# Chunked attention and a squared-ReLU layer in one kernel: the halves of x swapped, transposes, loads and the last product put at other steps

## The chip, the cores and the metric

The kernel runs on one core of a Trainium2 chip. The metric is the device time of one execution in microseconds, as a median over runs. Five engines work beside each other: TensorE (PE; its weight loads are listed as PEld), VectorE (DVE), ScalarE (ACT), GpSimd (POOL), and SyncE (SP), which here only issues transfers. Each engine takes its instructions strictly in the order of its own queue.

## The reference

Attention within chunks of 64 rows, then a feed-forward layer with a squared ReLU. Inputs and output are float32.

```
q, k, v: (8, 8, 576, 64)          # batch, heads, rows, width
scores = q_c @ k_c.T / 8          # inside each chunk of 64 rows
attn   = exp(scores - max) / sum
x      = (attn @ v_c), heads side by side    # (4608, 512)
h      = max(x @ w_in, 0)         # w_in (512, 2048)
out    = (h * h) @ w_out          # w_out (2048, 512), out (4608, 512)
```

## The kernel before

The 4608 rows are cut into 18 groups g of 256 rows and 9 blocks j of two groups (block j holds groups 2j and 2j+1). Groups 0 to 13, 16 and 17 are four neighbouring chunks of one batch; groups 14 and 15 (block 7) gather the last chunk of every batch, so their loads and stores come in more pieces. Everything is computed in bfloat16 with float32 sums.

The whole order is written out by hand. A table `plan` maps a step ("slot") to the functions that are called there; each engine's queue gets its instructions in the order of these calls. The work on one group has short names: its loads (`qk_pieces`, `v_pieces`, issued on SP), C(g) casts q and k to bfloat16 (L435, on POOL or ACT), TD(g) transposes them by one DMA on SP (L443), SC(g) makes the scores on PE and the exponential on ACT (L451), AV(g), or AV0(g) and AV1(g) for its two tiles, multiplies by V on PE and divides by the sums on DVE (L483, `out_of_x` L427: a reciprocal and a multiplication), and XT(g) transposes x into the block's tile `xT` (L517). XT is eight PE transposes and a copy up to group 11, and one DMA transpose on SP from group 12 on (`FIRST_DMA_X`). `xT` of a block has two halves of 256 rows; group 2j goes into half 0 and group 2j+1 into half 1.

Blocks 0 to 3 compute x @ w_in plainly (`ffn_in`, L559): 16 steps of four matmuls, each followed by a ReLU on ACT and a square on DVE or ACT. In block 2 the steps ("slots") 0 to 15 are these; AV(7) stood at slot 14, XT(6) after it at slot 14, XT(7) at slot 17. Slots 14 and 15 also hold the DVE sums of `g` for the second layer of block 2.

Blocks 4 to 8 use a scheme with seven products instead of eight, in quads Q (a quarter of the features of a block each): Q = 0 to 3 is block 4, Q = 12 to 15 block 7, Q = 16 to 19 block 8. Each tick of the loop `run` (L1125) has four steps s = 4*tick + i, so a block has 16 steps; block 7 begins at s = 48. The seven products of a quad are spread over two ticks:

```
groups = (((tick, "A1"), (tick - 1, "A7")), ((tick, "B2"), (tick - 1, "C3")),
          ((tick, "A6"), (tick - 1, "A4")), ((tick, "C5"),))
```

They read sums of the halves of x, which DVE makes (`x_sums`, L607): e1 is read by A1, e2 by A6, e3 by C5, e4 by A4; B2, C3 and A7 read x itself. With `xs(j, d, t)` for half t of x (d is the half of its features):

```
e1 = xs(j,0,1) - xs(j,1,1)      e2 = e1 + xs(j,0,0)
e3 = e2 - xs(j,1,0)             e4 = xs(j,0,1) + xs(j,0,0)
```

The sums of block j+1 are called in block j at its steps 13.5, 15, 17.5 and 18. e1 reads half 1 alone, e2 both halves.

The second layer is `ffn_out` (L713), also with seven products of 16 matmuls each; A and BC are its two accumulators. p1 multiplies a DVE sum d4 of `g` (d4 = g(0,1) - g(0,0)) by b21, p2 multiplies the plain piece g(0,0). The further DVE sums d5 (read by the third product), d3 (by the fourth) and d2 (by the seventh) are called after the half products K5, K2, K3 = 0, 1, 4. For blocks before the last the half products lie between the quads of the next block; those of the last block (the tail) run by themselves at the end. `keep` copies an accumulator away on ACT, `summed_out` (L801) adds on DVE and stores.

Block 6 calls, at its steps 0 to 14, one load each of block 8: six of q and k, then nine of V. It also calls XT(14) at 11.5, XT(15) at 12, C(16) and C(17) at 9 and 13, TD(16) and TD(17) at 12 and 13.5.

Of the kernel before, what the change touches and what calls it, by code (L numbers as in the profile page):

```python
# [144 lines left out]
def kernel(  # L145
# [22 lines left out]
    blocks = [[g, g + 1] for g in range(0, n_grp, 2)]  # L168
    n_blk = len(blocks)
# [7 lines left out]
    def is_whole(g):  # L177
        return chunks[g][0][0] == chunks[g][3][0]
# [5 lines left out]
    QUADS = 4  # L184
    LEAD = 4

    K5, K2, K3 = 0, 1, 4
    K5L, K2L, K3L = 2, 5, 5
# [97 lines left out]
    for g in range(n_grp):  # L286
        if is_whole(g):
# [3 lines left out]
            b, s = chunks[g][0]  # L291
# [47 lines left out]
    state = {}  # L339
    banks = {}  # L340

    def x_tile(j):
        if j not in xTs:
            xTs[j] = att_pool.tile([128, BT // 128, n_dt, 128], BF16, name="xT", bufs=2)
        return xTs[j]
# [170 lines left out]

    def transpose_x(g):  # L517
        x = state.pop(("x", g))
        dst = x_tile(g // 2)[:, g % 2 * 2:g % 2 * 2 + 2].rearrange("p t h q -> p (t h) q")
        if g >= FIRST_DMA_X:  # L520
            nc.sync.dma_start_transpose(out=dst, in_=x.rearrange("p t h a d -> p (t h a d)"))
            return
        psb = att_bank().bitcast(BF16)[:, 0:1024].rearrange("p (b q) -> p b q", q=128)
        for t in range(2):
            for hp in range(n_hp):
                nc.tensor.transpose(  # L526
                    out=psb[:, t * n_hp + hp, :],
                    in_=x[:, t, hp].rearrange("p a d -> p (a d)"),
                    identity=ident)
        copy = nc.vector.tensor_copy if g == blocks[1][0] else nc.scalar.copy  # L530
        copy(out=dst, in_=psb)  # L531
# [5 lines left out]
    for j in range(n_blk):  # L537
        if j < QUADS:
            at = {(th, fh, h): 4 * th + 2 * fh + h
                  for th in range(2) for fh in range(2) for h in range(2)}  # L540
        else:
# [6 lines left out]
            at = {(*key, 0): s for key, s in zip(keys, old)}  # L548
# [164 lines left out]
    def ffn_out(j):  # L713
# [4 lines left out]
        last = j == n_blk - 1  # L718
# [57 lines left out]
            return kept_sb[state["kept"] % 2]  # L776

        def store(dma, o_sb, half, col, t=None):
            g = blocks[j][half]
            b, s0 = chunks[g][0]  # L780
            t0 = b * S + s0
            if not is_whole(g):

                for p in range(2):
                    dma.dma_start(
                        out=out.rearrange("(b s) d -> s b d", s=S)[
                            s0:s0 + CH, b + p:b + 4:2, col:col + HD],
                        in_=o_sb[p * CH:(p + 1) * CH].rearrange("p (t d) -> p t d", d=HD))
            elif t is None:
                dma.dma_start(  # L790
                    out=out[t0:t0 + GT, col:col + HD].rearrange("(t p) d -> p t d", p=128),
                    in_=o_sb.rearrange("p (t d) -> p t d", d=HD))
            else:
                dma.dma_start(
                    out=out[t0 + t * 128:t0 + (t + 1) * 128, col:col + HD],
                    in_=o_sb[:, t * HD:(t + 1) * HD])
# [23 lines left out]
        def half(n):  # L820
            if early:
                return
            if n == (K5L if plain_first else K5):
                g_sum(d5, j, (1, 1), d4, ALU.subtract)
            if n == (K2L if plain_first else K2):
                g_sum(d2, j, (0, 1), (1, 1), ALU.subtract)
            if n == (K3L if plain_first else K3):
                g_sum(d3, j, (1, 0), d5, ALU.subtract)

        p1 = product(A, d4, b21, True)  # L830
        p2 = product(BC, (0, 0), b11_p_b21, True)
        order = (p2, p1) if plain_first else (p1, p2)
        for i, p in enumerate(order):
            for t in range(2):
                next(p)
# [142 lines left out]
    for j in range(QUADS):  # L978
        grps, nxt, far = blocks[j], blocks[j + 1], blocks[j + 2]
        plan = {}  # L980

        def at(slot, f, *x):
            plan.setdefault(slot, []).append((f, x))

        if j == 0:
            loads, go_slots = pieces(far), range(17)
            at(28, summed(b11_p_b21, b11, b21))
            for slot, f in ((24, TA), (27, SC), (29, AV), (31, XT)):
                at(slot, f, nxt[0])
            at(31, TQ, nxt[1])  # L990
            at(31, summed(b22_m_b21, b22, b21, ALU.subtract))
            phases = [first_ffn_in, ffn_out_by_ft(0)]
        elif j == 1:
            loads, go_slots = itertools.chain(*map(qk_pieces, far)), range(26, 48)
            for slot, f in ((1, TK), (4, SC), (7, AV), (12, XT)):
                at(slot, f, grps[1])
            for i, g in enumerate(nxt):
                for slot, f in ((16 + 4 * i, C), (21 + 4 * i, TD), (36 + i, SC), (38 + 2 * i, AV),
                                (41 + 2 * i, XT)):
                    at(slot, f, g)  # L1000
            for i, g in enumerate(far):
                at(36 + 4 * i, C, g)
                at(42 + 3 * i, TD, g)
            at(2, summed(b12_p_b21, b12, b21))
            at(12, summed(b11_m_b12, b11, b12, ALU.subtract))
            at(20, summed(b12_p_b22, b12, b22))
            out_j = ffn_out(1)
            for i in (20, 27, 29, 31):
                at(i, lambda: next(out_j)())
            phases = [ffn_in(1, [(0, 256, FT_ORDER), (256, 256, FT_ORDER)]), out_j]  # L1010
        else:
            out_j = ffn_out(j)
            for i in (14, 15):
                at(i, lambda: next(out_j)())
            phases = [ffn_in(j, [(0, BT, range(n_ft))])]
            if j == 2:
                loads, go_slots = itertools.chain(*map(v_pieces, nxt), pieces(far)), [
                    *range(16), *range(27, 36)]
                slots = {SC: (6, 9), AV: (11, 14), XT: (14, 17), C: (21, 26), TD: (25, 29)}
                for f in (C, TD):  # L1020
                    for i, g in enumerate(far):
                        at(slots[f][i], f, g)
                phases.append(out_j)
            else:
                loads, go_slots = pieces(far), range(11)
                for f, slots in ((C, (11, 13)), (TD, (13, 15))):
                    for i, g in enumerate(far):
                        at(slots[i], f, g)
                slots = {SC: (2, 4), AV: (7, 10), XT: (13, 15)}
            for f in (SC, AV, XT):  # L1030
                for i, g in enumerate(nxt):
                    at(slots[f][i], f, g)
            if j == 2:
                for i, f in enumerate((summed(a21_p_a22, a21, a22),
                                       summed(a12_m_a21, a12, a21, ALU.subtract),
                                       summed(a11_p_a21, a11, a21))):
                    at(1 + 2 * i, f)
        slot = 0
        for phase in phases:
            for _ in phase:  # L1040
                if slot in go_slots:
                    for f in loads:
                        f()
                        break
                for f, x in plan.get(slot, []):
                    f(*x)
                slot += 1
        assert all(x < slot for x in plan), (j, slot, sorted(plan))
        if j < QUADS - 1:
            go(loads)  # L1050
# [19 lines left out]
    for j in range(QUADS, n_blk):  # L1070
# [26 lines left out]
        if j + 1 < n_blk:  # L1097
            S0, V0, V1, X0 = ((1.5, 3.5), (4.5, 7.5), (6, 9.5), (8.5, 11.5)) if j == QUADS else (
                (0.5, 7), (2, 8), (3.5, 9.5), (3.5, 10)) if is_whole(blocks[j + 1][0]) else (
                (3.5, 9), (5, 10), (7, 11.5), (11.5, 12))  # L1100
            for i, g in enumerate(blocks[j + 1]):
                at(j, S0[i], SC, g)
                at(j, V0[i], AV0, g)
                at(j, V1[i], AV1, g)
                at(j, X0[i], XT, g)
            if j + 2 == n_blk:
                at(j, 22, check_sums)
                at(j, 25.5, count_bad)
            for i, s in enumerate((13.5, 15, 17.5, 18)):
                at(j, s, x_sums, j + 1, i)  # L1110
# [3 lines left out]
            assert next(loads, None) is None  # L1114
        if j + 2 < n_blk:
            more = pieces(blocks[j + 2])
            for s in range(0, 16):
                at(j, s, load, 1 if is_whole(blocks[j + 2][0]) else 2, more)
            for i in range(2):
                at(j, (9, 13)[i], C, blocks[j + 2][i])  # L1120
                at(j, (12, 13.5)[i], TD, blocks[j + 2][i])
    tail = ffn_out(n_blk - 1)
    at(n_blk, 3, lambda: next(tail)())

# [63 lines left out]
```

## Time and profile before

| | |
|---|---|
| median of 3 runs | 288.05 us (287.52 to 288.37) |
| profiled execution | 287.81 us, of it 286.0 us span |
| PE busy | 269.3 us (94%) |
| DVE, ACT, POOL busy | 199.1, 166.0, 91.8 us |
| mean granted PE clock | 0.991 |

The profiled execution is one run of the program on the chip. Its span goes from the first to the last instruction; 1.81 us lie around it. PE is nearly always busy, so an edit counts where it takes away or adds PE idle time, or time in which PE's clock is granted only in part. In the rows of the timeline view the columns are start, duration (from the first start to the last end of a merged run), engine, line, operation, destination and sources, and in brackets the idle time ahead of it and what ended it. SPq, POOLq and ACTq are the issue of a transfer, not its flight.

### The profile page before, as it was taken

To read this page: it belongs to the slowest core of one execution; us is meant where nothing else is said; L and a number is where in the kernel's file an instruction comes from. 1 tells how busy PE (TensorE), PEld (TensorE's weight loads), DVE (VectorE), ACT (ScalarE), POOL (GpSimd) and SP (SyncE) were. 2 spreads that over 40 slices of the span, in tenths; PEclk is the share of its full clock that TensorE was granted. 3 is DMA by queue.
4 is the path that set the end of the run, shared out by engine and by line. 5 is a ranking of instruction groups with operands and counts; after the bars stand their busy time and mean duration, and the time that the engine had idled before them with its cause. 6 is when DMAs were issued, how large, how long until landed. Compare 5 with 4: busy or idle time off the path is not lost.

```text
span 286.0 us, 7983 instructions
## 1 busy us (share of the span) xinstructions
PE 269.3 (94%) x3291; PEld 205.6 (72%) x3291; DVE 199.1 (70%) x367; ACT 166.0 (58%) x296; POOL 91.8 (32%) x123
## 2 busy tenths in 40 slices
PE   2999999999999799999999999999969999999994
PEld 2774445788764478447879888888847888888783
DVE  1276515999537671599989997789638877994841
ACT  1537614894458664875778666575626654766320
POOL 2047733240450001141245344522612322431612
PEclk9999999999999999999999999999988999999998
DMA  7999999989999976999998997798997320220313
GB/s 220 241 312 388 389 307 274 328 196 168 300 190 232 239 149 145 279 239 189 227 236 175 218 218 182 145 220 193 267 175 170 76 70 6 87 62 7 94 55 112
DMA packets 135480, 55.61 MB, mean 194 GB/s; under 512 B 104272, under 2 KB 131152, under 8 KB 135440
## 3 DMA queue, kind: packets, MB, share of 16 engines
q1 hardware_dynamic: 132432, 45.76, 69.3%
q0 software_dynamic: 2864, 9.18, 9.8%
q8 instruction: 27, 0.44, 0.6%
q10 hardware_dynamic: 144, 0.13, 0.1%
q14 instruction: 13, 0.11, 0.1%
HBM read 36.70 MB, written 9.44 MB: 161 GB/s over the span
## 4 chain that ended last, share of the span: by engine, by line
PE 81%; DVE 7%; DMA 4%; ACT 3%; SPq 3%; issue 1%; ACTq 0%
PE ps_ffn L642 20%; PE ps_out L761 19%; PE ps_ffn L565 15%; PE ps_ffn L761 13%; PE ps_ffn L877 5%; DMA qk_st<-in_k_dram 3%; DVE gT L583 2%; PE ps_att L470 2%; PE ps_att L497 2%; DVE x L432 2%; SPq L279 2%; PE ps_ffn L422 1%; PE ps_att L526 1%; DVE w_st L599 1%; PE ps_ffn L389 1%
## 5 line engine op out<-in xcount | busy, mean ns | idle before, releaser
L565 PE MATMUL ps_ffn<-xT,w_in_bf 128*128 128x512 bf16 (+1 forms) x328 | 58.7, 333 | 0.4 <-DVE xT L531 0.2
L761 PEld LDWEIGHTS <-w_st 128*128 128x128 bf16 x512 | 49.1, 98 | 8.3 <-DVE w_st L599 1.6
L650 DVE CUSTOM_DVE_ANT_0 relu<-ps_ffn,w_st 128x512 f32<-128x512 f32 x60 | 39.4, 684 | 14.5 <-PE ps_ffn L642 13.1
L583 DVE TENSOR_TENSOR gT<-relu 128x256 bf16<-128x256 bf16 (+2 forms) x69 | 33.7, 516 | 20.3 <-ACT relu L576 19.9
L576 ACT ACTIVATE relu<-ps_ffn 128x256 bf16<-128x256 f32 (+2 forms) x82 | 39.9, 503 | 11.7 <-PE ps_ffn L565 10.1
L565 PEld LDWEIGHTS <-w_in_bf 128*128 128x128 bf16 x328 | 30.9, 98 | 21.6 <-DVE xT L531 0.4
L642 PE MATMUL ps_ffn<-qk_st,w_in_bf 128*128 128x256 bf16 x240 | 35.3, 273 | 2.8 <-DVE qk_st L599 2.8
L790 POOL DMA_DIRECT2D out_dram<-o_sb x27 | 19.8, 733 | 53.1 <-DVE o_sb L599 52.0
L642 PEld LDWEIGHTS <-w_in_bf 128*128 128x128 bf16 x320 | 30.8, 98 | 7.3 <-DVE qk_st L599 3.1
L761 PE MATMUL ps_out<-w_out_bf,w_st 128*128 128x256 bf16 x240 | 31.0, 273 | 0.4 <-DVE w_st L599 0.4
L761 PEld LDWEIGHTS <-gT 128*128 128x128 bf16 x296 | 28.6, 98 | 3.4
L684 ACT ACTIVATE w_st<-ps_ffn 128x512 f32<-128x512 f32 x20 | 11.9, 597 | 25.8 <-PE ps_ffn L642 25.8
L481 ACT ACTIVATE e<-ps_att 128x1024 bf16<-128x1024 f32 x18 | 18.4, 1024 | 13.4 <-PE ps_att L470 13.4
L432 DVE TENSOR_TENSOR x<-ps_att,recs 128x512 bf16<-128x512 f32 x36 | 24.9, 691 | 1.2
L642 PEld LDWEIGHTS <-qk_st 128*128 128x128 bf16 x240 | 22.8, 99 | 3.1
L642 PE MATMUL ps_ffn<-xT,qk_st 128*128 128x256 bf16 x160 | 24.4, 277 | 0.0
L661 POOL TENSOR_TENSOR qk_st<-relu 128x512 bf16<-128x512 f32 x10 | 10.3, 1034 | 41.7 <-DVE relu L650 41.7
L661 POOL TENSOR_TENSOR gT<-relu 128x512 bf16<-128x512 f32 x10 | 10.3, 1034 | 41.4 <-DVE relu L650 37.6
L761 PE MATMUL ps_ffn<-w_out_bf,w_st 128*128 128x256 bf16 x144 | 17.6, 273 | 0.3 <-DVE w_st L599 0.3
L659 ACT ACTIVATE gT<-relu 128x512 bf16<-128x512 f32 x28 | 17.7, 633 | 0.0
L438 POOL CAST qkb<-qk_st 128x1024 bf16<-128x1024 f32 x12 | 12.6, 1048 | 15.0 <-DMA qk_st<-in_q_dram 15.0
L599 DVE TENSOR_TENSOR w_st<-gT,w_st 128x1024 bf16<-128x1024 bf16 x26 | 17.3, 700 | 0.0
(91 smaller groups left out, 430.8 us busy)
## 6 DMA issues: line engine op xcount, KB each, us to landing
qk_st<-in_q_dram SPq DMA_DIRECT2D x16, 512.0 KB, 5.4
out_dram<-o_sb POOLq DMA_DIRECT2D x31, 256.0 KB, 4.1
qk_st<-in_k_dram SPq DMA_DIRECT2D x24, 256.0 KB, 5.6
ve_sb<-in_v_dram SPq DMA_DIRECT2D x32, 128.0 KB, 4.0
w_st<-in_moe_w_in_dram SPq DMA_DIRECT2D x8, 512.0 KB, 6.5
w_st<-in_moe_w_out_dram SPq DMA_DIRECT2D x8, 512.0 KB, 5.5
vo_sb<-in_v_dram SPq DMA_DIRECT2D x24, 128.0 KB, 3.4
qk_st<-in_k_dram SPq DMA_DIRECT2D x4, 512.0 KB, 5.9
```

The costliest lines, as they stand in the source:

```text
L432: nc.vector.tensor_tensor(out=x, in0=o[:, :, :, 0:D], in1=rec.to_broadcast([128, 2, n, D]), op=ALU.mult)
L481: nc.scalar.activation(out=e_out, in_=s_in, func=AF.Exp, scale=scale)
L565: nc.tensor.matmul(out=h[:, 0:n], lhsT=w_in_bf[:, dt, ft * 128:(ft + 1) * 128], rhs=xT[:, c // 128:(c + n) // 128, dt, :], start=(dt == 0) ...
L576: nc.scalar.activation(out=rl[:, 0:n], in_=h[:, 0:n], func=AF.Relu)
L583: nc.vector.tensor_tensor(out=dst, in0=src, in1=src, op=ALU.mult)
L599: nc.vector.tensor_tensor(out=out, in0=in0, in1=in1, op=op)
L642: nc.tensor.matmul(out=bank[:, f * GT:(f + 1) * GT], lhsT=a[:, dt, ft * 128:(ft + 1) * 128], rhs=b[:, :, dt, :], start=(first and f == 0 a ...
L650: nc.vector._custom_dve(TENSOR_ADD_SAT, out=out, in0=in0, in1=in1, s0=BIG, s1=0.0)
L659: engine.activation(out=dst, in_=r, func=AF.Square)
L661: engine.tensor_tensor(out=dst, in0=r, in1=r, op=ALU.mult)
L761: nc.tensor.matmul(out=out_ps, lhsT=lhsT, rhs=b[:, i, :], start=(first and i == 0 and (last or t == 0)), stop=(i == HF - 1), skip_group_ch ...
L790: dma.dma_start(out=out[t0:t0 + GT, col:col + HD].rearrange("(t p) d -> p t d", p=128), in_=o_sb.rearrange("p (t d) -> p t d", d=HD))
```

## The change

`half_of(g)` puts group 2j into half 1 and group 2j+1 into half 0 from block 4 on; the stores follow. In block 2 AV(7) moves to slot 15, and XT(7) to slot 24. In block 6 XT(14) moves from step 11.5 to 7.5, TD(16) from 12 to 9.5, and the nine loads of V of block 8 from steps 6 to 14 to steps 10 to 15.5, two of them between TD(16) and XT(15), seven behind XT(15). In the last block p2 is computed ahead of p1, and d3 and d2 are called after the half products 4 and 5 (d2 before: 1).

```diff
+    def half_of(g):
+        return g % 2 if g // 2 < QUADS else 1 - g % 2
...
     def transpose_x(g):
         x = state.pop(("x", g))
-        dst = x_tile(g // 2)[:, g % 2 * 2:g % 2 * 2 + 2].rearrange("p t h q -> p (t h) q")
+        n = 2 * half_of(g)
+        dst = x_tile(g // 2)[:, n:n + 2].rearrange("p t h q -> p (t h) q")
...
         def store(dma, o_sb, half, col, t=None):
-            g = blocks[j][half]
+            g, = (g for g in blocks[j] if half_of(g) == half)
...
         def half(n):
             if early:
                 return
-            if n == (K5L if plain_first else K5):
+            k5, k2, k3 = (K5L, K2L, K3L) if plain_first else (0, 5, 4) if last else (K5, K2, K3)
+            if n == k5:
                 g_sum(d5, j, (1, 1), d4, ALU.subtract)
-            if n == (K2L if plain_first else K2):
+            if n == k2:
                 g_sum(d2, j, (0, 1), (1, 1), ALU.subtract)
-            if n == (K3L if plain_first else K3):
+            if n == k3:
                 g_sum(d3, j, (1, 0), d5, ALU.subtract)
...
-        order = (p2, p1) if plain_first else (p1, p2)
+        order = (p2, p1) if plain_first or last else (p1, p2)
...
             if j == 2:
-                slots = {SC: (6, 9), AV: (11, 14), XT: (14, 17), C: (21, 26), TD: (25, 29)}
+                slots = {SC: (6, 9), AV: (11, 15), XT: (14, 24), C: (21, 26), TD: (25, 29)}
...
             S0, V0, V1, X0 = ((1.5, 3.5), (4.5, 7.5), (6, 9.5), (8.5, 11.5)) if j == QUADS else (
                 (0.5, 7), (2, 8), (3.5, 9.5), (3.5, 10)) if is_whole(blocks[j + 1][0]) else (
-                (3.5, 9), (5, 10), (7, 11.5), (11.5, 12))
+                (3.5, 9), (5, 10), (7, 11.5), (7.5, 12))
...
             more = pieces(blocks[j + 2])
-            for s in range(0, 16):
-                at(j, s, load, 1 if is_whole(blocks[j + 2][0]) else 2, more)
+            if j == n_blk - 3:
+                for s, n in ((0, 1), (1, 1), (2, 1), (3, 1), (4, 1), (5, 1), (10, 2), (12.5, 3),
+                             (14, 1), (14.5, 1), (15, 1), (15.5, 1)):
+                    at(j, s, load, n, more)
+            else:
+                for s in range(0, 16):
+                    at(j, s, load, 1 if is_whole(blocks[j + 2][0]) else 2, more)
             for i in range(2):
                 at(j, (9, 13)[i], C, blocks[j + 2][i])
-                at(j, (12, 13.5)[i], TD, blocks[j + 2][i])
+                at(j, ((9.5, 13.5) if j == n_blk - 3 else (12, 13.5))[i], TD, blocks[j + 2][i])
```

## The prediction

> **What bounds the kernel now.** I read the page first, then PE's own waits, then the chain of waits and the timeline around the longest.
>
> ```profile
> span 286.0 us, 7983 instructions
> ...
> PE 269.3 (94%) x3291; PEld 205.6 (72%) x3291; DVE 199.1 (70%) x367; ACT 166.0 (58%) x296; POOL 91.8 (32%) x123
> ...
> PE ps_ffn L389 <- DMA qk_st<-in_q_dram: 4.7, 1, 4.7
> PE ps_ffn L642 <- DVE qk_st L599: 2.8, 1, 2.8
> PE ps_att L526 <- DVE x L432: 1.8, 1, 1.8
> ```
>
> PE fills 94% of the span, so only its gaps can be won. The longest, 4.7 us, is the first load, which the change leaves alone. The next two are single places: 2.8 us in the quads, 1.8 us before a PE transpose of x. Here is the first, on PE's timeline, in the chain of waits and in the windows view (whose last three columns are granted clock, DMA share, GB/s):
>
> ```profile
> 208.19 0.60 PE L761 MATMUL ps_out<-w_out_bf,qk_st 128*128 128x256 bf16 x4
> 211.63 0.61 PE L642 MATMUL ps_ffn<-qk_st,w_in_bf 128*128 128x256 bf16 x4 [2.84 <-DVE qk_st L599]
> ...
> 207.97 3.15 DMA xT<-x
> 211.14 0.44 DVE qk_st L599
> ...
> 212.67 1.62 PE ps_out L761 x8
> 214.29 1.71 PE ps_ffn L642 x8
> ...
> 217.38 0.87 PE ps_out L761 x8
> ...
> 210.00:214.00 4.00, 2.37 (x16) 1.91 (x17) 2.05 (x4) 1.12 (x2) 0.39 (x1) 0.83 1.01 190
> 214.00:218.00 4.00, 4.00 (x58) 2.94 (x56) 3.34 (x6) 1.52 (x3) 2.06 (x3) 0.74 1.00 218
> ```
>
> This is step 48, the start of block 7. A1 of quad 12 reads e1 (a slice of `qk_st`), DVE makes e1 from half 1 of x, and half 1 is group 15, whose DMA transpose XT(15) started at 207.97 and took 3.15 us. Eight matmuls cost 0.87 us at full clock, so four cost 0.44 and A1 was due at 208.19 + 0.44 = 208.63. It started at 211.63: 3.00 us lost. Then the clock was granted at 0.83 and 0.74, and two runs of eight took 1.62 and 1.71 instead of 0.87: another 0.75 + 0.84 = 1.59. This place costs 4.6 us. The DMA share of 1.00 to 1.01 says why XT(15) came late: the 16 DMA engines are full, and SP works its queue off behind them.
>
> **Block 6, and the swapped halves.** SP's timeline of block 6, with POOL's last cast of C(16), and the durations of all DMA transposes of q and k (TD: shortest, median, longest):
>
> ```profile
> 198.48 1.89 SPq L279 DMA_DIRECT2D qk_st<-in_k_dram  x2
> 200.41 1.95 SPq L307 DMA_DIRECT2D ve_sb<-in_v_dram  x2
> 202.41 2.08 SPq L311 DMA_DIRECT2D vo_sb<-in_v_dram  x3
> 204.53 1.20 SPq L307 DMA_DIRECT2D ve_sb<-in_v_dram  x1
> ...
> 205.90 1.97 SPq L521 DMA_TRANSPOSE xT<-x  x1
> ...
> 207.97 1.25 SPq L521 DMA_TRANSPOSE xT<-x  x1
> ...
> 209.96 2.91 SPq L447 DMA_TRANSPOSE qkT<-qkb  x1
> ...
> L447 SPq DMA_TRANSPOSE qkT<-qkb x14: 1724/2699/4429, 63.1 to 213.6; - x14
> ...
> 200.54 1.04 POOL L441 CAST qkb<-qk_st 128x1024 bf16<-128x1024 f32 x1 [1.85 <-DMA qk_st<-in_k_dram]
> ...
> vo_sb<-in_v_dram SPq DMA_DIRECT2D x24, 128.0 KB, 3.4
> ```
>
> Before, six loads of V (200.41 to 205.73) stood ahead of XT(14) and XT(15), and e1 needed the later of the two. With the change the order behind the last k load (200.37) is XT(14), TD(16), two loads of V, XT(15), three of V, TD(17), four of V. XT(14) then starts at 200.4 instead of 205.90; even at 4 us it has landed by 204.5, and with the halves swapped it is all that e1, A1 and B2 need, against 208.63. So the 3.00 us and the clock's 1.59 us go.
>
> Next late is XT(15), now the second operand of e2, with TD(16) ahead of it. 200.41 + 1.97 (XT(14)) = 202.38; TD(16) needs its casts, which ended at 201.58, 0.8 us before. TD(16) takes 2.70 by the median (1.72 to 4.43), two V loads 1.95: XT(15) starts at about 207.0, lands 3.15 later at 210.2 (209.2 to 211.9). PE needs e2 in A6 after A1, A7, eight of `ps_out`, B2, C3 (three times 0.87) and SC(16) (about 0.5): 208.63 + 3.1 = 211.7, or 211.2 with what block 2 wins below. That is met. But e2 stands in DVE's queue ahead of the work that follows it:
>
> ```profile
> 204.91 1.29 DVE L650 CUSTOM_DVE_ANT_0 relu<-ps_ffn,w_st 128x512 f32<-128x512 f32 x2 [0.47 <-PE ps_ffn L642]
> ...
> 212.09 0.41 DVE L599 TENSOR_TENSOR qk_st<-qk_st,xT 128x512 bf16<-128x512 bf16 x1
> ```
>
> Behind e2 (0.41) come the ReLU of A7, an output sum, the ReLUs of B2 and C3 (0.65 each by the pair above) and e3 (0.41): e3 is ready 3.3 us after XT(15) lands, at 213.5. C5 reads it, due about 2.0 us after A6 (two runs of 0.87 and about 0.3 for AV0(16)): 213.25. So PE waits 0.25 us there (0 to 2.0 over the range). The V of group 16 that AV0(16) needs is issued by 209.6 and lands after 3.4, at 213.0, just when AV0(16) comes; I add 0.15. Residue: 0.4 us. The four last V loads and TD(17) belong to group 17, eight steps later. TD(16), at 202.4, lands before SC(16) at 211. The swap itself costs nothing: the same sums, and the stores only change names. What it does to blocks 4, 5, 6 and 8 lies beside PE work, since PE has no wait for x there.
>
> [...]
>
> **Block 2.** AV(7) moves behind slot 14's XT(6), XT(7) to slot 24 between the third and fourth output products.
>
> ```profile
> 98.53 0.62 PE L526 MATMUL ps_att<-ident,x 128*128 128x128 bf16 x8 [1.79 <-DVE x L432]
> ...
> 104.63 1.91 PE L761 MATMUL ps_ffn<-w_out_sum,w_st 128*128 128x256 bf16 x16 [0.67 <-ACT kept L818]
> 106.38 1.91 PE L761 MATMUL ps_ffn<-w_out_bf,w_st 128*128 128x256 bf16 x16
> ...
> 100.74 0.42 DVE L583 TENSOR_TENSOR gT<-relu 128x512 bf16<-128x512 bf16 x1 [1.42 <-ACT relu L576]
> ...
> 101.80 2.49 DVE L599 TENSOR_TENSOR w_st<-gT,w_st 128x1024 bf16<-128x1024 bf16 x4
> 104.21 1.28 DVE L599 TENSOR_TENSOR w_st<-gT 128x1024 bf16<-128x1024 bf16 x2
> ...
> 97.07 0.63 ACT L581 ACTIVATE gT<-relu 128x512 bf16<-128x512 bf16 x1
> 99.19 1.01 ACT L531 COPY xT<-ps_att 128x1024 bf16<-128x1024 bf16 x1 [1.49 <-PE ps_att L526]
> ...
> L432 DVE TENSOR_TENSOR x<-ps_att,recs 128x512 bf16<-128x512 f32 x36 | 24.9, 691 | 1.2
> ```
>
> Before, XT(6) waited 1.79 us for the bank that DVE read for AV(7). Now it takes a free bank, and its ACT copy follows the square that ends at 97.70, 1.5 us sooner, and ends at 98.6. But two new waits appear. AV(7)'s second tile takes the bank that this copy (1.01 us) empties: about 0.9 us of PE idle. And AV(7)'s four DVE operations now queue behind the sums d4, d5, d3, d2. Those start when the last square is done (100.74 before, about 1.5 us earlier now), take 7 halves of about 0.62 us, to about 103.9, and the four operations 1.7 us more (0.69 for each of the two multiplications, the rest reciprocals): x of group 7 is ready at 105.6. XT(7) is due at 104.8 (98.6, 0.15 for AV(7)'s tile, three products of 1.75, and 0.8 for the kept copy) and, held by x, ends at 105.9. That wait (0.67 in its row, with the hand-over 0.8) is there before and after. So the fourth product starts at about 105.9 instead of 106.38: 0.5 us won (bounds: 0.9 if XT(7) finds x ready, -0.4 if DVE runs a microsecond later). The copy of XT(7) moves past C(8)'s casts on ACT, which start earlier for it; TD(8) follows them and has over 10 us before SC(8).
>
> **The tail.**
>
> ```profile
> 267.10 1.91 PE L761 MATMUL ps_out<-w_out_bf,w_st 128*128 128x256 bf16 x16
> ...
> 269.36 2.08 PE L761 MATMUL ps_ffn<-w_out_bf,w_st 128*128 128x256 bf16 x16 [0.35 <-DVE w_st L599]
> ...
> 271.28 0.60 PE L761 MATMUL ps_ffn<-w_out_sum,qk_st 128*128 128x256 bf16 x4
> ...
> 271.48 0.37 ACT L818 COPY kept<-ps_ffn 128x256 f32<-128x256 f32 x1 [0.50 <-PE ps_ffn L761]
> ...
> 273.29 0.42 DVE L599 TENSOR_TENSOR o_sb<-ps_ffn,kept 128x256 f32<-128x256 f32 x1 [0.46 <-PE ps_ffn L761]
> ```
>
> Sixteen matmuls take 1.75 us (104.63 to 106.38 above), so p1 was due at 268.85 and came at 269.36, and it took 1.92: 0.68 us lost to d4. p2 needs no sum; its 1.75 us cover d4 whole. If p2's own operand were late, the cover would be gone and the 0.68 us be back. Given back: `summed_out` now waits for the copy of p1, and d3 stands behind it. After p1's end: 0.20 to the copy, 0.37, the addition 0.42, two halves of d3 at 0.64, and hand-overs, 2.4 us; the second half is read 1.75 + 0.44 = 2.2 us after. That is 0.2 lost, 0.5 won. d2 moved behind d3 is read three products later.
>
> **The sum.** 3.0 + 1.6 - 0.4 + 0.5 + 0.5 = 5.2 us off the profiled 287.81: 282.6. The median of the runs is 0.24 above the profiled one, so I forecast 282.8.
>
> **The rivals.** First: the wait moves from e1 to e2 and e3. For it: the DMA engines are full, and TD(16), twice XT's bytes, is now ahead of XT(15). Against: XT(15) is hardly later than before even at TD's longest, and what waits for it comes three microseconds later. At 4.43 us for TD(16) it lands at 211.9, C5 waits 2 us: 284.4. With the V loads slipping too, and a clock lowered again at about 3 us of idle (1.6), it ends near 286.5.
> [...] The rows of the transposes themselves say 2.70, which I take.
>
> Second, slower: SP stops at TD(16). It cannot pass an instruction that waits, so if the casts of group 16 end late, XT(15) and all V behind it are held, and DVE, and with it PE, behind e2. C5's wait is XT(15)'s landing minus 209.95. The whole gain is spent, the clock's 1.6 us included, when it is 4.0 us: landing at 213.95, TD(16) held 3.8 us. Held 5.1 us it costs 5.35 + 1.6: 289.4. For it: the casts follow k's landing by waits (1.85 us above). Against: they ended 0.8 us before SP comes, and nothing ahead of them changes.
>
> Third, no change: the halves swap as said but e1 remains behind a DVE instruction that waits, or the stall returns at about 4 us: 287.2 to 288.9.
>
> **How the numbers follow.** The forecast has 0.60 (281.6 with no residue and block 2's best, to 283.8), the first rival 0.22 (283.8 to 286.5), the third 0.06, slower 0.12. The range for 8 in 10 is 281.6 to 286.5. A measurement of this kernel can tell about 0.3%, 0.86 us, from no change; so faster 0.82, same 0.06, slower 0.12.
>
> **What would show it.** Right: no PE wait of L642 for `qk_st` at step 48, the clock at 1.00 through 206 to 214, XT(14) issued right behind the k loads and some 5 us before XT(15); a DVE wait for `xT` that remains, before e2; the L526 wait of 1.8 split into smaller ones; the tail's first `ps_ffn` product without a wait for `w_st`. Wrong: an L642 wait of over 1 us for `qk_st` at A6 or C5, a clock under 1, SP idle ahead of TD(16), or PE waiting at AV0(16) for `vo_sb`.

## The result, and the profile after

| | before | after |
|---|---|---|
| median of 13 runs | 287.8 us (285.24 to 288.82) | 284.8 us (283.72 to 286.27) |
| ratio | | 0.992, interval 0.989 to 0.9949 |
| profiled execution, span | 287.81, 286.0 us | 284.43, 282.7 us |
| mean granted PE clock | 0.991 | 1.0 |

The kernel became faster: the interval of the ratio lies under 1. The forecast time was 2.0 us too low, and the forecast ratio was 282.8 / 288.05 = 0.982; by the measured ratio less than half of that gain came. The ratio is the recorded one, of fast runs alone; the quotient of the medians is 0.990. A second measurement of the same kernel, in another batch, gave 0.9871 (0.982 to 0.9922), so the gain is known only as 0.8 to 1.3%.

Line numbers after L339 moved by 4 to 6 with the change: L642 is now L647, L761 L766, L599 L604, L521 L526, L447 L451. The page and PE's own waits of the changed kernel:

```profile
span 282.7 us, 7975 instructions
...
PE 267.3 (95%) x3288; PEld 204.7 (72%) x3291; DVE 199.3 (71%) x367; ACT 166.2 (59%) x296; POOL 93.5 (33%) x123
...
PE ps_ffn L647 <- DVE qk_st L604: 2.4, 3, 1.3
PE ps_att L501 <- ACT xT L536: 0.9, 2, 0.7
PE ps_ffn L766 <- ACT kept L823: 0.7, 1, 0.7
...
PE ps_att L531 <- DVE x L436: 0.2, 1, 0.2
```

The one wait of 2.8 us on the sums of x became three of 2.4 us together. The 1.8 us of block 2 became 0.9 and 0.2. This is the start of block 7 on PE's timeline, and the clock there (the column ahead of the last two):

```profile
207.08 0.60 PE L766 MATMUL ps_out<-w_out_bf,qk_st 128*128 128x256 bf16 x4
208.45 0.61 PE L647 MATMUL ps_ffn<-qk_st,w_in_bf 128*128 128x256 bf16 x4 [0.77 <-DVE qk_st L604]
...
211.17 0.45 PE L474 MATMUL ps_att<-qkT 64*64 64x64 bf16 x32
212.90 0.61 PE L647 MATMUL ps_ffn<-qk_st,qk_st 128*128 128x256 bf16 x4 [1.28 <-DVE qk_st L604]
...
215.62 0.60 PE L647 MATMUL ps_ffn<-qk_st,w_in_bf 128*128 128x256 bf16 x4 [0.40 <-DVE qk_st L604]
...
210.00:214.00 4.00, 2.72 (x53) 2.06 (x51) 1.58 (x4) 1.69 (x3) 0.47 (x1) 1.00 1.04 189
214.00:218.00 4.00, 3.60 (x57) 2.88 (x59) 3.97 (x10) 2.74 (x6) 1.98 (x3) 1.00 1.11 254
```

A1 was due at 207.08 + 0.44 = 207.52 and came 0.93 us late; A6 was due 0.38 us after SC(16) began and came 1.35 late; C5 came some 0.45 late. That is 2.7 us where 0.4 was forecast and 4.6 was lost before. The clock stayed at 1.00. SP's timeline and the chain of waits say what PE waited for:

```profile
197.56 1.82 SPq L279 DMA_DIRECT2D qk_st<-in_k_dram  x2
199.56 2.27 SPq L526 DMA_TRANSPOSE xT<-x  x1
201.92 5.35 SPq L451 DMA_TRANSPOSE qkT<-qkb  x1
207.32 1.13 SPq L307 DMA_DIRECT2D ve_sb<-in_v_dram  x2
208.55 1.24 SPq L526 DMA_TRANSPOSE xT<-x  x1
...
199.56 8.38 DMA xT<-x
...
208.55 3.77 DMA xT<-x
...
207.96 0.43 DVE L604 TENSOR_TENSOR qk_st<-xT 128x512 bf16<-128x512 bf16 x1 [1.83 <-DMA xT<-x]
...
212.42 0.42 DVE L604 TENSOR_TENSOR qk_st<-qk_st,xT 128x512 bf16<-128x512 bf16 x1 [3.43 <-DMA xT<-x]
```

The order on SP is as forecast; the durations are not. TD(16) held SP for 5.35 us, so XT(15) was issued only at 208.55 and landed at 212.32. XT(14), issued at 199.56, took 8.38 us. e1 (the DVE row at 207.96) and e2 (212.42) each started when their transpose had landed.

Block 2 and the tail, on PE's timeline:

```profile
95.77 0.65 PE L531 MATMUL ps_att<-ident,x 128*128 128x128 bf16 x8
...
98.24 0.22 PE L501 MATMUL ps_att<-ve_sb,e 64*64 64x65 bf16 x2 [0.70 <-ACT xT L536]
...
105.22 0.40 PE L531 MATMUL ps_att<-ident,x 128*128 128x128 bf16 x4 [0.25 <-DVE x L436]
105.46 1.91 PE L766 MATMUL ps_ffn<-w_out_bf,w_st 128*128 128x256 bf16 x16
...
264.25 1.91 PE L766 MATMUL ps_out<-w_out_bf,w_st 128*128 128x256 bf16 x16
...
271.24 2.02 PE L766 MATMUL ps_ffn<-w_out_bf,w_st 128*128 128x256 bf16 x16
...
278.54 0.42 DVE L873 COPY o_sb<-ps_ffn 128x256 f32<-128x256 f32 x1 [1.32 <-PE ps_ffn L766]
```

From XT(6) to the fourth output product block 2 takes 9.69 us; before, from AV(7) at 96.28 to 106.38, it took 10.10. From the last `ps_out` product to the last copy the tail takes 14.29 us; before, 267.10 to 281.96, 14.86. The fourth product of the tail takes 2.02 instead of 1.91 us: the wait for d3.

So the profile accounts for 1.9 us at block 7, 0.4 in block 2 and 0.6 in the tail. The remaining half microsecond of the 3.4 us between the two profiled executions was there before block 2's change began (95.77 against 96.28).

### The profile page after: what moved, and what is told of

Same layout as the page of the kernel before. It is cut to its first block, busy times and chain, and to the rows that moved or that the text cites. A ratio compares the mean times of both kernels' runs of the same rounds, so it can differ in the third digit from the quotient of the medians.

```text
span 282.7 us, 7975 instructions
## 1 busy us (share of the span) xinstructions
PE 267.3 (95%) x3288; PEld 204.7 (72%) x3291; DVE 199.3 (71%) x367; ACT 166.2 (59%) x296; POOL 93.5 (33%) x123
## 4 chain that ended last, share of the span: by engine, by line
PE 76%; DMA 10%; DVE 8%; ACT 2%; issue 1%; SPq 1%; DVEq 0%; ACTq 0%
PE ps_ffn L647 19%; PE ps_out L766 18%; PE ps_ffn L570 14%; PE ps_ffn L766 11%; PE ps_ffn L883 5%; DMA xT<-x 4%; DMA qk_st<-in_k_dram 4%; DVE w_st L604 2%; PE ps_att L474 2%; PE ps_att L501 2%; DVE gT L588 2%; DMA qkT<-qkb 2%; DVE x L436 2%; PE ps_ffn L426 1%; PE ps_att L531 1%
## 5 line engine op out<-in xcount | busy, mean ns | idle before, releaser
L766 PEld LDWEIGHTS <-w_st 128*128 128x128 bf16 x512 | 49.0, 98 | 7.3 <-issue 0.8
L647 PE MATMUL ps_ffn<-qk_st,w_in_bf 128*128 128x256 bf16 x240 | 35.3, 273 | 1.2 <-DVE qk_st L604 1.2
L647 PEld LDWEIGHTS <-w_in_bf 128*128 128x128 bf16 x320 | 30.6, 98 | 5.6 <-DVE qk_st L604 1.0
L766 PE MATMUL ps_out<-w_out_bf,w_st 128*128 128x256 bf16 x240 | 31.0, 273 | 0.1
L766 PEld LDWEIGHTS <-gT 128*128 128x128 bf16 x296 | 28.5, 98 | 3.4
L647 PEld LDWEIGHTS <-qk_st 128*128 128x128 bf16 x240 | 22.6, 98 | 4.3 <-DVE qk_st L604 1.4
L647 PE MATMUL ps_ffn<-xT,qk_st 128*128 128x256 bf16 x160 | 23.9, 273 | 0.0
L442 POOL CAST qkb<-qk_st 128x1024 bf16<-128x1024 f32 x12 | 13.5, 1124 | 14.1 <-DMA qk_st<-in_q_dram 14.1
L766 PE MATMUL ps_ffn<-w_out_bf,w_st 128*128 128x256 bf16 x144 | 17.5, 273 | 0.0
L445 POOL CAST qkb<-qk_st 128x1024 bf16<-128x1024 f32 x12 | 14.6, 1215 | 8.4 <-DMA qk_st<-in_k_dram 8.4
```

The source lines that it names most:

```text
L445: copies[1](out=qkb[:, 1], in_=loaded(g, 1))
L647: nc.tensor.matmul(out=bank[:, f * GT:(f + 1) * GT], lhsT=a[:, dt, ft * 128:(ft + 1) * 128], rhs=b[:, :, dt, :], start=(first and f == 0 a ...
L766: nc.tensor.matmul(out=out_ps, lhsT=lhsT, rhs=b[:, i, :], start=(first and i == 0 and (last or t == 0)), stop=(i == HF - 1), skip_group_ch ...
```

## The experiments

What has to be told apart: why XT(14) and XT(15) came so late. Theory A: TD(16), which held SP for 5.35 us where XT(14) held it for 2.27, stretches XT(14) from right behind it and holds SP ahead of XT(15). Theory B: the loads of q and k just ahead of XT(14) are the cause. A third question is what each part of the change gives by itself. Each batch has its own runs of the kernel before.

**TD(16) back behind XT(15)** (the changed kernel, one edit):

```diff
-                at(j, ((9.5, 13.5) if j == n_blk - 3 else (12, 13.5))[i], TD, blocks[j + 2][i])
+                at(j, (12, 13.5)[i], TD, blocks[j + 2][i])
```

> The changed kernel with TD(16) back at step 12, so that SP issues XT(14), two V loads, XT(15), TD(16). Theory A (a long transpose right behind a short one holds it up, and holds SP): XT(14) lands about 4 us after its issue instead of 8.4, A1's wait of 0.8 us goes; XT(15) is issued at about 203.5 and lands by 207.5, so the waits at A6 and C5 (1.3 and 0.4 us) go too; but SC(16) may wait up to 1 us for TD(16). Time 2 us under the changed kernel. Theory B (XT(14) is slow because of the q and k loads issued just ahead of it): XT(14) lands 7 to 8 us after its issue, A1's wait stays at 0.5 to 0.9 us; XT(15) comes earlier all the same, and 1 to 1.5 us are won.

Measured: 284.23 us against 288.74, ratio 0.9854 (0.9815 to 0.9892). SP's timeline, and PE's only wait between 205 and 217:

```profile
202.40 2.58 SPq L526 DMA_TRANSPOSE xT<-x  x1
205.02 1.43 SPq L307 DMA_DIRECT2D ve_sb<-in_v_dram  x2
206.55 1.49 SPq L526 DMA_TRANSPOSE xT<-x  x1
208.14 2.73 SPq L451 DMA_TRANSPOSE qkT<-qkb  x1
210.92 1.83 SPq L311 DMA_DIRECT2D vo_sb<-in_v_dram  x3
212.85 4.21 SPq L451 DMA_TRANSPOSE qkT<-qkb  x1
...
PE ps_att L474 <- DMA qkT<-qkb: 0.8, 1, 0.8
```

XT(14) landed 5.9 us after its issue, between the two theories. XT(15) was issued 4.15 us after XT(14), where the changed kernel needed 8.99. A1, A6 and C5 wait for nothing, and SC(16) waits 0.8 us for TD(16), as expected. Moving TD(16) forward was what made XT(15) late. SP's whole time for these entries changed less than their order: from the two k loads ahead of XT(14) to the end of the last of XT(14), XT(15), TD(16) and the two V loads it took 11.0 us here and 12.2 us in the changed kernel (197.56 to 209.79). The last row, TD(17) behind three loads of V, took 4.21 us; it matters below. By time this version is not clearly apart from the changed kernel, whose ratio was 0.992 and 0.9871 in other batches.

**TD(16) one step later, behind two loads of V but still ahead of XT(15):**

```diff
-                at(j, ((9.5, 13.5) if j == n_blk - 3 else (12, 13.5))[i], TD, blocks[j + 2][i])
+                at(j, ((10.5, 13.5) if j == n_blk - 3 else (12, 13.5))[i], TD, blocks[j + 2][i])
```

> The changed kernel with TD(16) one step later, at 10.5: SP issues XT(14), two V loads, TD(16), XT(15). Only what follows XT(14) at once differs from the changed kernel. Theory A (the long transpose on its heels stretches XT(14) from about 6 to 8.4 us): XT(14) lands about 6 us after its issue, A1 waits for nothing; XT(15) stays behind TD(16), is issued at about 208 and lands near 212, so A6 still waits 1 us. The time lies 0.5 to 1 us under the changed kernel. Rival (XT(14) is slow only because of the k loads ahead): XT(14) again at 8 us, A1's wait stays, time as the changed kernel.

Measured: 285.41 us against 289.13, ratio 0.9894 (0.9836 to 0.9951); not told apart from the changed kernel by time. SP's timeline and PE's row of A6:

```profile
201.85 3.04 SPq L526 DMA_TRANSPOSE xT<-x  x1
204.94 1.55 SPq L307 DMA_DIRECT2D ve_sb<-in_v_dram  x2
206.59 3.41 SPq L451 DMA_TRANSPOSE qkT<-qkb  x1
210.09 1.25 SPq L526 DMA_TRANSPOSE xT<-x  x1
...
213.79 0.61 PE L647 MATMUL ps_ffn<-qk_st,qk_st 128*128 128x256 bf16 x4 [1.52 <-DVE qk_st L604]
```

XT(14) landed after 6.7 us, and A1 still waited 0.6, which I had not expected. XT(15) came at 210.09, and A6 waited 1.5 us. So here the neighbour of XT(14) isn't what costs most, but that XT(15) stands behind TD(16) at all.

**The changed kernel itself again:**

> The changed kernel itself, on the same chip as the other runs of this batch. If block 7's start is the term that was mis-sized, its trace repeats what the first showed: XT(14) 7 to 9 us from issue to landing, TD(16) over 4 us on SP, A1, A6 and C5 waiting 2 to 3 us together, no lowered clock; ratio to before 0.988 to 0.993.

Measured: 285.61 us against 289.13, ratio 0.9871 (0.982 to 0.9922). XT(14) took 7.8 us, TD(16) held SP for 4.85 us, XT(15) was issued at 209.09. PE's waits for the sums of x were 1.2 us together, half of the first profile's and less than the 2 to 3 us that I expected: PE reached A1 at 209.2 and found e1 ready; A6 waited 0.79 us and C5 0.40. The late transposes repeat; the wait at A1 does not.

**The change without the swap** (`half_of(g)` returns `g % 2`):

> The change without the swap of the halves: block 6's new order, block 2 and the tail as in the change, but e1 again needs half 1 = group 15. XT(15) landed at 212.3 in the changed kernel, later than the 211.1 before. By my reading A1 then waits some 5 us, the clock is lowered again (about 1.6 us), and the whole is as slow as before or up to 1 us slower (ratio 0.995 to 1.005, the tail and block 2 giving back 1 us). By the rival, that the swap matters little beside the order on SP, it is within 1 us of the changed kernel.

Measured: 289.72 us against 289.13, ratio 1.002 (0.9993 to 1.0048): no gain is left, as expected. PE's row of A1, and two stages:

```profile
213.04 1.03 PE L647 MATMUL ps_ffn<-qk_st,w_in_bf 128*128 128x256 bf16 x4 [4.28 <-DVE qk_st L604]
...
210.00:214.00 4.00, 0.96 (x5) 0.72 (x6) 1.36 (x3) 0.00 (x0) 0.00 (x0) 0.87 0.99 200
214.00:218.00 4.00, 4.00 (x56) 2.92 (x55) 2.08 (x4) 1.23 (x3) 2.12 (x3) 0.70 0.94 183
```

A1 waited 4.28 us for XT(15), and the clock fell to 0.87 and 0.70. With the change's order on SP the swap is needed.

**The swap alone** (the kernel before with `half_of`), twice:

> The kernel before with the halves swapped and nothing else. e1 then needs XT(14), which landed at about 210.0 before, instead of XT(15) at 211.1: A1's wait falls from 3.0 to about 1.5 us, no lowered clock follows, and e2 follows at 211.5. By my reading of the stall the time falls by 2 to 3 us against the kernel before, so the swap alone gives as much as the whole change at this place. By the rival (the wait goes to e2 and the sums behind it) it falls by under 1 us.

> The swap of the halves alone, once more: its first profile had a wait of 3.6 us at SC(14), at another place than the one asked about. If the swap moves the wait on e1 to XT(14), as I read it, A1 waits 0 to 1.5 us, the clock stays at 1.00, and the next wait is e2's or SC(16)'s at 1 us: the start of block 7 costs 1.5 to 2.5 us instead of 4.6. Time 1 to 2.5 us under the kernel before. The rival says under 1 us.

Measured: 287.43 against 288.74 us, ratio 0.9966 (0.9936 to 0.9996), and 287.51 against 288.25, 0.9971 (0.9936 to 1.0006): by the ratios 1.0 and 0.8 us, as the rival said; the intervals reach 1.8 us, short of my 2 to 3 but not of the 1 to 2.5 of the second try. The first profile, of a run of 290.38 us, had a wait of 3.6 us at SC(14), for TD(14), and says nothing of step 48. The second, PE's timeline at A1 and the stage:

```profile
208.49 0.60 PE L766 MATMUL ps_out<-w_out_bf,qk_st 128*128 128x256 bf16 x4
211.05 0.61 PE L647 MATMUL ps_ffn<-qk_st,w_in_bf 128*128 128x256 bf16 x4 [1.97 <-DVE qk_st L604]
...
210.00:214.00 4.00, 2.95 (x17) 2.21 (x18) 2.14 (x4) 1.11 (x2) 0.72 (x1) 0.72 1.05 210
```

With XT(14) in its old place e1 came only a little earlier (DVE began it at 210.57 us against 211.14 before), and in this profile PE waited 1.97 us and the clock was lowered all the same (0.72). But this is the smaller part of the runs: 16 of the 24 runs of the swap alone had a mean granted clock of 0.996 or more, against 13 of 63 runs of the kernel before. So the swap alone keeps the clock more often than not, as I had read it, and still wins only about 1 us. Kept clocks in so many more runs, at some 1.5 us each, are 0.7 us by estimate, most of that gain.

**The tail alone:**

> The kernel before with the tail's new order alone. The profile should show the tail 0.5 to 0.6 us shorter from the end of block 7's last output product to the end (14.9 us before: 267.10 to 281.96), with no wait of PE for w_st ahead of the first ps_ffn product and about 0.1 us ahead of the fourth. The time falls by about 0.5 us, less than its interval may show.

Measured: 288.35 against 288.74 us, ratio 0.9977 (0.994 to 1.0015). The first row is the last `ps_out` product, the second the last copy:

```profile
267.59 1.91 PE L761 MATMUL ps_out<-w_out_bf,w_st 128*128 128x256 bf16 x16
...
281.88 0.42 DVE L868 COPY o_sb<-ps_ffn 128x256 f32<-128x256 f32 x1 [1.32 <-PE ps_ffn L761]
```

The tail took 14.29 us, 0.57 under before, exactly as in the changed kernel. The time alone can't show it.

**Block 2 alone:**

> The kernel before with block 2's steps alone. From the start of XT(6) or AV(7) behind the 60th matmul of block 2 to its fourth output product it should take 9.7 us instead of 10.1 (as in the changed kernel: 95.77 to 105.46 against 96.28 to 106.38). The time falls by 0.4 us; that, or nothing, since the loads that set the start of block 7 do not come earlier and the wait there may take it back.

Measured: 288.08 against 288.25 us, ratio 1.0006 (0.9976 to 1.0037): no gain that the time shows, though its interval reaches 0.7 us. The stretch in block 2 took 9.69 us (95.47 to 105.16), the 0.4 us are there; but PE still stops at step 48, for the same transpose:

```profile
206.97 0.60 PE L761 MATMUL ps_out<-w_out_bf,qk_st 128*128 128x256 bf16 x4
209.94 0.61 PE L642 MATMUL ps_ffn<-qk_st,w_in_bf 128*128 128x256 bf16 x4 [2.37 <-DVE qk_st L599]
```

Whether the wait takes the 0.4 us back is not shown. In this profile it did not grow: A1 came 104.78 us after the fourth product of block 2, and 105.25 us in the kernel before.

**A better order: XT(14) ahead of the loads of group 17, TD(16) behind XT(15)** (the changed kernel; the first list with V ahead of XT(15), the second with all V of group 16 behind TD(16)):

```diff
-                for s, n in ((0, 1), (1, 1), (2, 1), (3, 1), (4, 1), (5, 1), (10, 2), (12.5, 3),
+                for s, n in ((0, 1), (1, 1), (2, 1), (8, 1), (8.5, 1), (9, 1), (10, 2), (12.5, 3),
...
-                for s, n in ((0, 1), (1, 1), (2, 1), (3, 1), (4, 1), (5, 1), (10, 2), (12.5, 3),
+                for s, n in ((0, 1), (1, 1), (2, 1), (8, 1), (8.5, 1), (9, 1), (12.5, 5),
...
-                at(j, ((9.5, 13.5) if j == n_blk - 3 else (12, 13.5))[i], TD, blocks[j + 2][i])
+                at(j, (12, 13.5)[i], TD, blocks[j + 2][i])
```

> The changed kernel with TD(16) back at step 12 and the three q and k loads of group 17 at steps 8 to 9, behind XT(14). SP: q and k of 16, XT(14) at about 196, q and k of 17, two V loads, XT(15), TD(16). Both theories: XT(14) lands by 204 and A1 waits for nothing. Theory A: XT(14) lands 4 to 5 us after its issue. Theory B: 7 to 8 us after, for the k loads of 16 lie just ahead. The casts of group 17 start some 2 us later on POOL, which has nothing due then. Time 2 to 3 us under the changed kernel (282 to 283).

> Candidate for the fastest: XT(14) ahead of the loads of group 17, then XT(15), TD(16), and all V of group 16 behind TD(16). SP waits for x of group 15 until about 203.5, issues XT(15) then and TD(16) at about 205, landing by 210. e1 and e2 find their x landed, and SC(16)'s wait of 0.5 us of the run with the V loads ahead goes. Against it: V of 16 lands at about 213, when AV0(16) comes, which may wait up to 0.5 us. Time 0 to 0.5 us under that run, 2 to 3 us under the changed kernel.

> The fastest version once more, in another batch: no wait at the start of block 7, ratio to before 0.978 to 0.987.

Measured: the first list 283.88 against 288.74 us, 0.9859 (0.9817 to 0.99); XT(14) landed after 5.3 us, SC(16) waited 0.5. The second list 283.93 against 289.13, 0.9821 (0.9772 to 0.9871), and again 284.97 against 288.25, 0.987 (0.9822 to 0.9918). In the second list's first profile PE waits for nothing from 202 to 218 (4.00 us busy in each 4 us); in its second profile AV0(16) waits 0.2 us for V, the cost that I had named. Between the two lists the time decides nothing.

**The second list without the swap:**

> The order XT(14), loads of 17, XT(15), TD(16), V without the swap. XT(15) landed at 209.5 in the run with the swap, A1 was due at about 208.1: without the swap A1 waits 1.5 to 2 us, the clock stays. By my reading the swap is then worth 1.5 to 2 us even in this order; by the rival (the order on SP is all) under 0.5 us.

Measured: 283.45 against 288.25 us, ratio 0.9829 (0.9784 to 0.9874). SP, DVE and the stage:

```profile
204.63 2.02 SPq L526 DMA_TRANSPOSE xT<-x  x1
206.75 1.92 SPq L451 DMA_TRANSPOSE qkT<-qkb  x1
...
208.44 0.43 DVE L604 TENSOR_TENSOR qk_st<-xT 128x512 bf16<-128x512 bf16 x1 [1.71 <-DMA xT<-x]
...
206.00:210.00 4.00, 4.00 (x37) 3.37 (x36) 2.05 (x4) 2.63 (x5) 1.45 (x1) 1.00 1.10 168
```

My reading was wrong here and the rival right: XT(15), issued at 204.63, landed just ahead of A1 (208.92, due 208.78), and the swap is worth nothing measurable. I had set the second list's landing of XT(15) (209.5) against an A1 at 208.1, which is that of the first list (208.18); in the second list's own first profile A1 came at 209.82. In all three profiles of this order DVE finished x of group 15 4.18 us before A1 was due, and XT(15) was issued at once; it flew 3.8 us here, which left A1 0.14 us late. With the 4.3 us of the second list's second profile it would be some 0.6 us, by estimate. So the order on SP counts most here; the swap repairs an order that brings XT(15) late. This is the lowest median of all, but its interval overlaps those of the second list and of the changed kernel in its second batch, so the time does not settle that it beats the changed kernel; its trace lacks the changed kernel's waits of 1.2 to 2.7 us at step 48.

## Why the prediction was wrong, step by step

**The bound, right.** The stall at step 48 was where the time lay; the versions without a wait for e1 or e2 there (of over 0.2 us) gain 1.3 to 1.8%, the parts alone, which keep the old order of block 6, under 0.4%.

**XT(14) and e1: wrong in size.** The step "even at 4 us it has landed by 204.5" failed: XT(14) was issued at 199.56, but landed at 207.94, when A1 had been due at 207.52. It took 8.4, 7.8 and 6.9 us in the three profiles with TD(16) on its heels, 5.9 and 6.7 with V behind it after the k loads, 4.2 to 5.3 in the four with the loads of group 17 behind it, and 3.6 to 4.1 before and in the parts alone, behind V (5.7 in the first profile of the swap alone). So the q and k loads ahead cost about 2 us and TD(16) behind it 0.2 to 2.5 more: both theories hold a part, as far as one profile of each order can tell. I had taken a flight time measured behind loads of V and used it right behind loads of q and k. A1 came 0.9 us late.

**XT(15) and e2: the term that decided.** The step "TD(16) takes 2.70 by the median: XT(15) starts at about 207.0, lands at 210.2" failed. TD(16) held SP 5.35 us (4.85 and 3.70 in the two other profiles with this order on SP), longer than any such transpose of the kernel before (4.43). The two V loads took 1.13 instead of 1.95, which gave a little back; XT(15) flew 3.77 instead of 3.15 us. It landed at 212.32, 0.4 us outside my bounds, and e2 held A6 by 1.35 us. C5 then waited as the step's own rule says. An issue time that was read in one order is no price: here it changed with what SP had issued before. TD(16) took 5.35, 4.85 and 3.70 right behind XT(14), 3.41 with two V loads between, and 1.84 to 2.97 behind XT(15). The row that I took the median of said so already: its longest, 4.43, is TD(15), which stands right behind two loads of V that follow TD(14), and took 3.78 to 4.59 in every one of the 14 profiles.

**The clock: right for the changed kernel, its worth too high.** The residue came in pieces of 0.9, 1.35 and 0.45 us, and the clock stayed at 1.00; all 13 runs had a mean of 0.996 or more. But the sum takes the 1.6 us of one profile as lost in every run of the kernel before. In the batches of the experiments 13 of its 63 runs kept a mean clock of 0.999 or more, and these were on average 1.3 to 1.7 us faster than the others that the ratio counts. So the size holds, but it was there to be won in about four runs of five. And the sum's residue, as well as the wait of 2 us at C5 in the first rival's 284.4, is counted without a lowered clock. For a wait that long this is not safe: the 1.97 us wait in the profile of the swap alone was followed by a lowered clock (0.72 from 210 to 214 us).

**Block 2, right in the stretch.** 0.41 us against 0.5, with the waits named (0.70 for the bank, 0.25 for x, 0.67 for the kept copy). Whether it adds to the rest in the time, the runs can't resolve.

**The tail, right.** 0.57 us against 0.5, with the wait for d3 at 0.11 instead of 0.2.

**The rivals.** The first one, "the wait moves from e1 to e2 and e3", is what happened, with TD's length as its cause. It stood at 0.22 with 283.8 to 286.5; the 284.8 us lie there. The sum was 1.9 + 0.4 + 0.6 = 2.9 instead of 5.2: of the shortfall, 2.3 us are the residue at step 48. No run shows the term behind 283.8, the upper end of the forecast and the lower end of this rival; what the runs showed in its place is TD(16) holding SP for 1.84 to 5.35 us, so the row's 2.70 is no fixed price.

## What to carry to other kernels

The issue time of a transfer belonged to its place in the queue here: the same transpose, TD(16), held SP for 1.84 to 5.35 us. Price a moved transfer by its flight behind the same neighbours, or keep the whole spread, and put the transfer that is needed first at the head. Before swapping operands so that a late transfer is needed less, ask whether the queue can bring it earlier: here the order alone did as much (ratio 0.9829 without the swap, 0.9821 and 0.987 with it). And look at the clock of all runs before a stall's cost is taken from one profile: about one run in five of the kernel before (13 of 63) did not pay it.

## What the runs showed of the hardware that was not expected

The clock was lowered after shorter gaps than in the kernel before, where PE waited 2.84 us: PE waits at A1 of 1.97 us (the swap alone, second profile) and 2.37 us (block 2 alone) were followed by matmuls at half speed (0.72 and 0.59 granted from 210 to 214 us; four matmuls in 0.85 to 0.86 us instead of 0.44), while waits of 1.79 us (block 2, before; 1.00 granted from 98 to 102 us) and 1.52 us (TD(16) one step later; four matmuls in 0.44 us behind it) were not. Counted from the start of the last four matmuls to A1's start these two gaps were 2.6 and 3.0 us, that of the kernel before 3.4 us.

What made TD slow to issue is open. A short transpose just ahead of it was neither needed nor enough: TD(16) took 1.84 to 2.97 us right behind XT(15), while TD(15) took 3.78 to 4.59 us right behind two loads of V. What stood further ahead went with a difference: right behind the same three loads of V, TD(17) took 4.09 to 4.66 us where TD(16) stood ahead of them (five profiles) and 2.82 to 3.10 us where XT(15) did (four). TD(16) is twice XT(15) in bytes (two casts of 128x1024 in bf16 against two tiles of x of 128x512) and also flew longer (4.6 us against 3.15 in the kernel before, 7.5 against 3.77 in the changed one), so neither a fuller queue nor one transpose holding up the next is excluded. It wasn't tried with plain loads in TD(16)'s place.
